# Two convolution layers and two SwiGLU layers on one core: the first filter block in two transfers, weight sums in other buffers, and a new instruction order

## The chip, the core and the metric

The kernel runs on one core of a Trainium2 chip. The core has five engines that run at the same time, each with its own list of instructions: TensorE (PE in the profile, its weight loads PEld) multiplies matrices and transposes, VectorE (DVE) and ScalarE (ACT) work element by element, GpSimd (POOL) does small things, SyncE (SP) issues DMA transfers. An instruction waits for semaphores that other engines and transfers raise. TensorE writes to PSUM, eight banks of 128 x 512 fp32; all other tiles are in SBUF, 128 partitions wide.

The metric is the time of one execution in microseconds (us) on the device; a smaller one is better. A version is shown by the median of its runs. A profile is taken of one execution apart from these.

## The reference

Two kinds of layer alternate, A, B, A, B, with the same weights both times, on x of 2048 rows by 512 columns (bf16):

```python
def _A_ref(q, k, v, shift_k, ssm_k, ssm_D):      # S = 2048, D = 512
    k_shift = sum(k_pad[:, t:t + S] * shift_k[:, 3 - t] for t in range(4))
    kv = k_shift * v
    y = irfft(rfft(kv, 2 * S) * rfft(ssm_k, 2 * S))[:, :S]   # a causal convolution per column
    return q * (y + kv * ssm_D)
def _B_ref(x, w_gate, w_up, w_down):             # F = 1792
    return (silu(x @ w_gate) * (x @ w_up)) @ w_down
x = A_q
x = x + _A_ref(_layernorm(x), A_k, A_v, ...)
x = x + _B_ref(_layernorm(x), ...)
x = x + _A_ref(_layernorm(x), A_k, A_v, ...)
x = x + _B_ref(_layernorm(x), ...)
```

The convolution y does not depend on x: it is made once and used by both A layers.

## The kernel before

**Tiling.** The 2048 rows are four blocks c of 512; in a block, row 4p + r stands on partition p in slot r. The convolution is a block convolution in the frequency domain. For each block of the filter (h) and of kv, TensorE multiplies the four slots with a table of cosines and sines (`fwd`), VectorE combines the results in butterflies, multiplies spectra (`product`), and TensorE goes back with the transposed table `inv`. kv itself is made on TensorE for the first two blocks: k, transposed, times 16 diagonal matrices `dg` that hold the taps (`shift_mul`), and then a product with v on VectorE (L614, L605). The filter lies with its columns on partitions, so TensorE transposes it for blocks 0 and 1 (`transpose_h`, L567) into the tile hs, and DMA does it for blocks 2 and 3.

**Units.** An FFN unit is (layer, block, half of the block): 16 units of 256 rows. Ahead of a unit, `prologue` normalises x, adds the A layer, normalises again to z and has z transposed to zT, by a DMA (L980), and for the first unit by TensorE (L1008). A unit reads zT against `w_gate` and `w_up` (L400, banks pf), ScalarE takes silu and copies (L1113, L1114, L1173, L1177), VectorE multiplies both, and TensorE multiplies the result with `w_down` (L1200, banks pd). In five late units the down product goes by a scheme of seven products in place of eight (`seven`, L1075); for it VectorE forms five sums and differences of halves of `w_down` once (`weight_sums`, L1022), each 128 x 1792.

**Buffers.** Tiles come from rings (L376), each with a number of equal buffers: one for h, one for k, one for v, one for hs, 11 of 8 KB a partition in s8, and so on. A new tile waits until the last reader of the tile that held its buffer is through.

**Order.** All instructions are recorded first, some 1,700 steps of them. The list `ORDER` (L55) gives each step its rank, and they are emitted in that sequence, engine by engine; it was found by a search outside the kernel. `Plan.walk` estimates when each step runs. From this, `Plan.issue` puts 33 filler matmuls of 128 columns (`warm`, L1482), which compute nothing, into TensorE's early waits, where the estimate has a wait of over 0.5 us before a limit, 6.0 us; what is left of the 33 goes to the first such place. The start of SP's queue is h block 0 (L432), k (L442), v (L472), x (L476), h block 1, v block 1, `w_gate`; k is on TensorE's list behind h: 16 transposes for h (L567), 16 for k (L456), then the pairs of matmuls on hs and the shift matmuls with `dg`.

The start of SP's queue and of TensorE's list, as the program is built:

```
SP:  hn (512 KB), kn, vt, xc, hn block 1, vt block 1, wg_sb, inv x2, kTb, wu_sb, wd_sb, wd_sb, xc
PE:  21 wm, 4 taps, 12 wm, 4 x 4 h transposes, 16 k transposes, 8 on hs, 8 on dg, ...
```

Of the kernel before, what the change touches and what calls it, by code (L numbers as in the profile page):

```python
# [9 lines left out]
P = 128  # L10
# [36 lines left out]
H_SPLIT = False  # L47
# [75 lines left out]

PASSES, WARM, FETCH, PHASE, TOOK = 4, 33, 256, 173, 1.1

NS = 8
BLOCKS = [("C", 0, 1), ("C", 1, 1), ("C", 2, 1), ("C", 3, 1),
# [1389 lines left out]
```

## Time and profile before

| | us |
|---|---|
| median of 3 runs | 339.34 (339.18 to 339.55) |
| profiled execution | 340.1 |
| its span, first to last instruction | 338.3 |
| TensorE busy, of the span | 333.9 |
| VectorE busy | 299.8 |
| ScalarE busy | 265.0 |
| first FFN matmul starts | 33.22 |
| one matmul of 512, 256, 128 columns behind another | 0.216, 0.109, 0.056 |

The span holds all instructions of the program; the 1.8 us between it and the execution's time lie around it. A matmul's row shows more than its share (0.379 us for 512 columns), since the next one starts before it is done; so a time for many is taken from start to start. A step of the chain that ended last says when it began, for how long, engine, tile and line.

### The profile page before, as it was taken

How to read it: one execution, taken by the hardware profiler on the slowest of the kernel's cores; microseconds unless marked ns; L12 is line 12 of the kernel's file. 1: busy time of each engine (PE TensorE's matmuls, PEld its weight loads, DVE VectorE, ACT ScalarE, POOL GpSimd, SP SyncE). 2: the span in 40 equal slices, each digit the busy share in tenths (PEclk: the TensorE clock that was granted, in tenths of full speed). 3: DMA queues.
4: the chain of work that ended last, by engine and by line, in shares of the span. 5: the costliest groups of instructions: out<-in, count | busy, mean ns of one | idle time of the engine just before them, and what ended most of it. 6: DMA issues, size and time to landing. Idle time of an engine off the chain costs nothing.

```text
span 338.3 us, 5940 instructions
## 1 busy us (share of the span) xinstructions
PE 333.9 (99%) x2172; PEld 205.7 (61%) x2172; DVE 299.8 (89%) x508; ACT 265.0 (78%) x543; POOL 34.5 (10%) x48
## 2 busy tenths in 40 slices
PE   9999999999999999999999999999999999999996
PEld 8665865645454564745444564644546587867884
DVE  7899999999779997999999999989997967977465
ACT  6989999999987477989999886989765555566473
POOL 4010011003100000132030000101200010100000
PEclk9999999999999999999999999999999999999999
DMA  7999501443355336381333263510504230203201
GB/s 266 341 290 365 75 0 33 84 107 90 64 125 93 81 79 155 62 159 32 62 48 67 57 107 116 105 34 16 96 16 96 56 85 2 48 17 78 64 3 62
DMA packets 77992, 31.59 MB, mean 93 GB/s; under 512 B 69765, under 2 KB 75786, under 8 KB 77962
## 3 DMA queue, kind: packets, MB, share of 16 engines
q1 hardware_dynamic: 77808, 31.13, 39.8%
q8 instruction: 17, 0.28, 0.3%
q14 instruction: 13, 0.11, 0.1%
q10 hardware_dynamic: 154, 0.07, 0.1%
HBM read 12.33 MB, written 2.10 MB: 43 GB/s over the span
## 4 chain that ended last, share of the span: by engine, by line
PE 87%; ACT 7%; DVE 5%; issue 1%; POOL 0%; DVEq 0%; POOLq 0%
PE pf L400 50%; PE pd L1200 17%; PE ps L1075 7%; PE ps L400 7%; PE ps L548 2%; ACT jk L922 2%; PE wm L1485 1%; PE ps L879 1%; ACT sg L1113 1%; ACT hr L1114 1%; ACT X L509 1%; PE pt L567 1%; DVE t L746 1%; DVE m L630 1%; DVE Z L750 1%; DVE t L742 1%
## 5 line engine op out<-in xcount | busy, mean ns | idle before, releaser
L400 PEld LDWEIGHTS <-zT 128*128 128x128 bf16 x528 | 51.5, 98 | 59.4 <-DMA zT<-z 0.9
L400 PE MATMUL pf<-wu_sb,zT 128*128 128x512 bf16 x264 | 65.0, 379 | 0.0
L400 PE MATMUL pf<-wg_sb,zT 128*128 128x512 bf16 x264 | 64.9, 379 | 0.0
L1200 PE MATMUL pd<-wd_sb,sg 128*128 128x512 bf16 x200 | 49.4, 379 | 0.0
L1113 ACT ACTIVATE sg<-pf 128x512 bf16<-128x512 f32 x66 | 38.7, 604 | 11.4 <-PE pf L400 10.3
L400 PE MATMUL pf<-zT,wg_sb 128*128 128x256 bf16 x368 | 46.7, 273 | 0.0
L1114 ACT CAST hr<-pf 128x512 bf16<-128x512 f32 x66 | 38.2, 591 | 9.6 <-PE pf L400 9.0
L400 PE MATMUL pf<-zT,wu_sb 128*128 128x256 bf16 x368 | 45.4, 273 | 0.2 <-ACT zT L1013 0.2
L742 DVE TENSOR_TENSOR t<-X,G 128x4096 bf16<-128x4096 bf16 x18 | 41.0, 2280 | 0.1
L400 PEld LDWEIGHTS <-wg_sb 128*128 128x128 bf16 x368 | 36.0, 98 | 8.0
L400 PEld LDWEIGHTS <-wu_sb 128*128 128x128 bf16 x368 | 36.0, 98 | 7.1 <-issue 0.5
L1173 ACT ACTIVATE sg<-pf 128x512 bf16<-128x512 f32 x46 | 27.5, 606 | 10.9 <-PE pf L400 9.7
L1177 ACT CAST ht<-pf 128x512 bf16<-128x512 f32 x46 | 27.3, 599 | 10.8 <-PE pf L400 10.4
L889 POOL TENSOR_TENSOR rstd<-mv,nhalf 128x2 f32<-128x2 f32 x20 | 18.5, 928 | 160.3 <-DVE mv L899 160.3
L1200 PEld LDWEIGHTS <-sg 128*128 128x128 bf16 x200 | 19.6, 98 | 21.5
L1200 PE MATMUL pd<-wd_sb,ht 128*128 128x512 bf16 (+1 forms) x126 | 29.1, 369 | 0.0
L898 DVE BATCH_NORM_STATS2 bst<-xc 128x6 f32<-128x512 bf16 x40 | 26.4, 682 | 0.5
L1180 DVE TENSOR_TENSOR ht<-ht,sg 128x512 bf16<-128x512 bf16 (+1 forms) x31 | 16.7, 546 | 9.5 <-ACT sg L1173 6.2
L889 POOL TENSOR_TENSOR rstd<-ve,nhalf 128x2 f32<-128x2 f32 x12 | 12.4, 1032 | 112.3 <-ACT ve L926 112.3
L1120 DVE TENSOR_TENSOR hr<-hr,sg 128x1024 bf16<-128x1024 bf16 x27 | 18.4, 681 | 4.3 <-ACT hr L1114 2.3
L509 ACT ACTIVATE X<-ps 128x512 bf16<-128x512 f32 x32 | 18.8, 611 | 2.2 <-DVE Z L746 1.1
L1200 PEld LDWEIGHTS <-ht 128*128 128x128 bf16 x126 | 12.3, 98 | 12.8 <-ACT z L945 0.3
(143 smaller groups left out, 525.7 us busy)
## 6 DMA issues: line engine op xcount, KB each, us to landing
hn<-in_A_ssm_k_dram SPq DMA_DIRECT2D x4, 512.0 KB, 4.0
vt<-in_A_v_dram SPq DMA_DIRECT2D x4, 512.0 KB, 6.0
xc<-in_A_q_dram SPq DMA_DIRECT2D x4, 512.0 KB, 5.3
out_dram<-xc SPq DMA_DIRECT2D x15, 128.0 KB, 1.8
wg_sb<-in_B_w_gate_dram SPq DMA_DIRECT2D x1, 1792.0 KB
wu_sb<-in_B_w_up_dram SPq DMA_DIRECT2D x1, 1792.0 KB, 7.9
wd_sb<-in_B_w_down_dram SPq DMA_DIRECT2D x1, 1280.0 KB, 13.2
sg<-hr SPq DMA_TRANSPOSE x66, 2.4
```

What stands on the lines that cost most here:

```text
L400: nc.tensor.matmul(o, lhsT=lhsT, rhs=rhs, start=(n == 0), stop=(n == len(terms) - 1))
L509: add("ACT", act(D), lambda: nc.scalar.activation(out=view(), in_=ps.t[:], func=ACT.Copy, scale=scale), r=[ps], w=[(buf, keys)], conv=conv)
L742: dve(8 * D, lambda t=t, part=part: nc.vector.tensor_mul(out=t.t[:], in0=x.t[:, :, part:part + 1, :].to_broadcast((P, R, 2, D)), in1=g.t[: ...
L889: add("POOL", cost, lambda: nc.gpsimd.tensor_tensor(out=rstd.t[:], in0=var(), in1=nhalf.t[:].to_broadcast((P, n)), op=ALU.pow), r=reads + ...
L898: add("DVE", 0.6, lambda st=st, i=i: nc.vector.bn_stats(out=st.t[:, 0:6], in_=xs[c].t[:, i, :]), r=[(xs[c], (i,))], w=[st])
L1075: nc.tensor.matmul(bank.t[:, half_ * C:(half_ + 1) * C], lhsT=lhsT(i), rhs=rhs(i), start=(first and i == 0 and half_ == 0), stop=(last and ...
L1113: add("ACT", act(D), lambda ps=ps, dst=dst, o=o, which=which: nc.scalar.activation(out=rows(dst, o), in_=ps.t[:], func=ACT.Silu) if which ...
L1114: out=rows(dst, o), in_=ps.t[:], func=ACT.Silu) if which == "g" else nc.scalar.copy(out=rows(dst, o), in_=ps.t[:]),
L1120: dve(n * W, lambda: nc.vector.tensor_mul(out=hr.t[:], in0=hr.t[:], in1=sg.t[:]), [sg], [hr], due=(unit, k / pairs, 0.0, "h"))
L1173: add("ACT", act(D), lambda ps=ps, o=o, sg=sg: nc.scalar.activation(out=sg.t[:, o:o + 2, :], in_=ps.t[:], func=ACT.Silu), r=[ps], w=[(sg, ...
L1177: add("ACT", act(D), lambda ps=ps, o=o, ht=ht: nc.scalar.copy(out=ht.t[:, o:o + 2, :], in_=ps.t[:]), r=[ps], w=[(ht, (o // 2,))], due=(uni ...
L1200: nc.tensor.matmul((pds[o] if not cs.start else pds[HP]).t[:, cs], lhsT=ht.tiles(q, o), rhs=wt["d"].t[:, ft, cs], start=(ft == std0 and no ...
```

## The change

Three things are changed, and no computation is added or left out.

First, `H_SPLIT` is set: `load_h` issues block 0 of the filter as two transfers of two column blocks each (256 KB), and `transpose_h` turns each row slot in two steps of two transposes, so that the steps on one half need that half alone. The functions held this branch before.

Second, the sums of the down weights are five tiles in place of three, in the buffers of h, k, hs, the diagonals, and one of s8 (three of s8 before). The diagonals `dg` are a ring of one buffer for this.

Third, `Plan.walk` lets TensorE run at half rate before 5.4 us of its own time, the limit for filler matmuls is 32.0 in place of 6.0, and `ORDER` is another list.

```diff
-H_SPLIT = False
+H_SPLIT = True
...
 ORDER = [
-    1, 64, 179, 187, 2, 5, 0, 11, 15, 3, 4, 8, 14, 34, 36, 9, 7, 10, 6, 13,
+    4, 91, 145, 160, 1, 7, 5, 10, 25, 0, 3, 14, 2, 6, 58, 59, 11, 9, 12, 8,
...
-PASSES, WARM, FETCH, PHASE, TOOK = 4, 33, 256, 173, 1.1
+PASSES, WARM, FETCH, PHASE, TOOK, RAMP = 4, 33, 256, 173, 1.1, 5.4
...
             o.end = o.start + o.cost
+            if o.eng == "PE" and o.start < RAMP:
+                o.end += 0.48 * min(1.92 * o.cost, RAMP - o.start)
...
-    dg = whole("dg", [P, KD, KS, P], parts=KD * KS)
+    dg = new("dg", "dg", [P, KD, KS, P], parts=KD * KS)
...
-        a = ws["14"] = new("s8", "wsa", [P, 2, NF // 2, C], parts=2)
-        b = ws["3"] = new("s8", "wsb", [P, NF // 2, C])
-        c = ws["67"] = new("s8", "wsc", [P, NF, C])
...
+        a0, a1 = (new(ring, "wsa", [P, NF // 2, C]) for ring in ("h", "k"))
+        b = new("hs", "wsb", [P, NF // 2, C])
+        c0, c1 = (new(ring, "wsc", [P, NF // 2, C]) for ring in ("dg", "s8"))
+        ws.update({"1": a0, "4": a1, "3": b, "6": c0, "7": c1})
+        for out, x0, x1, op in ((a0, lambda: ev(lo), lambda: od(hi), ALU.add), (b, lambda: ev(hi), lambda: od(hi), ALU.subtract),
+                                (a1, lambda: od(lo), lambda: ev(lo), ALU.subtract), (c0, lambda: ev(lo), lambda: ev(hi), ALU.add),
+                                (c1, lambda: od(lo), lambda: od(hi), ALU.add)):
...
-        plan.issue(*plan.order(ORDER), 6.0, warm)
+        plan.issue(*plan.order(ORDER), 32.0, warm)
```

The built program has the same number of matmuls, of steps on ScalarE and of DMA transposes; SP issues one transfer more. Its start:

```
SP:  hn blocks 2-3, kn, hn blocks 0-1, vt, xc, hn block 1, vt block 1, wg_sb, inv x2, kTb, wu_sb, wd_sb, hn, vt, wd_sb, xc
PE:  22 wm, 4 taps, 5 wm, 8 h transposes, 8 h transposes, 16 k transposes, 10 on hs, 4 on dg, ... 1 on hs, 6 wm, 16 on dg, ...
```

More of the change, by code (lines that the diff above doesn't have):

```diff
@@ L374, in span @@
         return slice(rows[0], rows[-1] + 1, rows[1] - rows[0])
-    plan = Plan({"h": 1, "k": 1, "v": 1, "hs": 1, "x": 2, "y": 2, "s8":11, "n": 2, "jk": 1, "dn": 1, "ks": 2, "z": 3, "zT":3,
+    plan = Plan({"h": 1, "k": 1, "v": 1, "hs": 1, "dg": 1, "x": 2, "y": 2, "s8":11, "n": 2, "jk": 1, "dn": 1, "ks": 2, "z": 3, "zT":3,
                  "ht":7, "st": 4, "bn": BN_SLOTS, "mv": 9, "ve": 8, "rs": 6, "pf": 4, "pc": 2, "pd": 2, **RINGS})
@@ L1027, in weight_sums @@
         lo, hi = slice(0, C), slice(C, D)
-        a = ws["14"] = new("s8", "wsa", [P, 2, NF // 2, C], parts=2)
-        b = ws["3"] = new("s8", "wsb", [P, NF // 2, C])
-        c = ws["67"] = new("s8", "wsc", [P, NF, C])
-        for out, keys, x0, x1, op in (
-                (lambda: a.t[:, 0], [(a, (0,))], lambda: ev(lo), lambda: od(hi), ALU.add),
-                (lambda: b.t[:], [b], lambda: ev(hi), lambda: od(hi), ALU.subtract),
-                (lambda: a.t[:, 1], [(a, (1,))], lambda: od(lo), lambda: ev(lo), ALU.subtract)):
-            dve(NF // 2 * C, lambda out=out, x0=x0, x1=x1, op=op: nc.vector.tensor_tensor(out=out(), in0=x0(), in1=x1(), op=op),
-                [wd], keys)
-        for n in range(2):
-            sl = slice(n * NF // 2, (n + 1) * NF // 2)
-            dve(NF // 2 * C, lambda sl=sl: nc.vector.tensor_tensor(out=c.t[:, sl], in0=wd.t[:, sl, lo], in1=wd.t[:, sl, hi], op=ALU.add),
-                [wd], [c])
+        a0, a1 = (new(ring, "wsa", [P, NF // 2, C]) for ring in ("h", "k"))
[5 more added lines that the diff above has]
+                                (c1, lambda: od(lo), lambda: od(hi), ALU.add)):
+            dve(NF // 2 * C, lambda out=out, x0=x0, x1=x1, op=op: nc.vector.tensor_tensor(out=out.t[:], in0=x0(), in1=x1(), op=op),
+                [wd], [out])
     def strided(src, off, dims):
@@ L1060, in seven @@
         for bank, rd, terms in (
-                (e, [ht, ws["14"], ws["3"]], (
-                    (0, lambda i: ht.tiles(2 * i + 1, 1), lambda i: ws["14"].t[:, 1, f0 + i]),
+                (e, [ht, ws["4"], ws["3"]], (
+                    (0, lambda i: ht.tiles(2 * i + 1, 1), lambda i: ws["4"].t[:, f0 + i]),
                     (1, lambda i: ht.tiles(2 * i, 0), lambda i: ws["3"].t[:, f0 + i]))),
@@ L1066, in seven @@
                     (1, lambda i: cb.t[:, 1, i], lambda i: wd.t[:, 2 * (f0 + i), 0:C]))),
-                (r, [(cb, (1,)), ws["67"]], (
-                    (0, lambda i: cb.t[:, 3, i], lambda i: ws["67"].t[:, 2 * (f0 + i) + 1]),
-                    (1, lambda i: cb.t[:, 2, i], lambda i: ws["67"].t[:, 2 * (f0 + i)]))),
-                (o, [(cb, (2,)), ws["14"]], (
-                    (0, lambda i: cb.t[:, 4, i], lambda i: ws["14"].t[:, 0, f0 + i]),))):
+                (r, [(cb, (1,)), ws["6"], ws["7"]], (
+                    (0, lambda i: cb.t[:, 3, i], lambda i: ws["7"].t[:, f0 + i]),
+                    (1, lambda i: cb.t[:, 2, i], lambda i: ws["6"].t[:, f0 + i]))),
+                (o, [(cb, (2,)), ws["1"]], (
+                    (0, lambda i: cb.t[:, 4, i], lambda i: ws["1"].t[:, f0 + i]),))):
             def go(bank=bank, terms=terms):
```

128 rows, old and new, of the table ORDER are left out of this document.

## The prediction

> **What bounds the kernel now.** I read the page's table of engines first, then the chain of waits in order of time, then busy time by stretches, and last the timelines of the queues and of VectorE for the first 34 us.
>
> ```profile
> PE 333.9 (99%) x2172; PEld 205.7 (61%) x2172; DVE 299.8 (89%) x508; ACT 265.0 (78%) x543; POOL 34.5 (10%) x48
> ```
> ```profile
> 0.77 2.40 PE wm L1485 x21
> 3.39 1.39 PE wm L1485 x12
> 4.78 1.71 PE pt L567 x16
> 6.49 1.20 PE pt L456 x16
> 7.69 7.03 PE ps L400 x80
> ...
> 31.49 0.70 ACT ks L604
> 32.20 0.50 ACT Yk L799
> 32.70 0.48 ACT zT L1013
> 33.22 5.40 PE pf L400 x48
> ...
> 250.95 1.30 DVE Z L647 x2
> 252.29 0.61 PE ps L400 x2
> ...
> 333.96 1.32 PE pd L1200 x12
> ```
> ```profile
> 31.30:34.00 2.70, 2.22 (x19) 1.35 (x19) 2.53 (x5) 2.70 (x7) 0.00 (x0) 1.00 1.06 364
> 34.00:335.30 301.30, 301.17 (x1872) 182.59 (x1869) 269.65 (x436) 235.54 (x482) 28.87 (x30) 1.00 0.34 68
> 335.30:338.30 3.00, 0.00 (x0) 0.00 (x0) 0.21 (x1) 0.37 (x1) 0.00 (x0) 0.96 0.41 125
> ```
>
> TensorE is the bound, and its work is fixed. The groups by shape give 978 matmuls 512 wide, 973 of 256 and 217 of 128; back to back they start 0.216, 0.109 and 0.056 us apart, so 211 + 106 + 12 = 329.4 us. The span of 338.3 is 0.8 before the first one, 329.4, a tail of 3.2 behind the last, and 4.9 in which TensorE starts nothing. Of these 4.9, about 3.0 are the start: until 7.0 us the matmuls stand 0.107 apart instead of 0.056 (1.71 us for 16 transposes; the same 16 take 0.9 later). About 1.0 is the hole before the first FFN matmul: the chain leaves TensorE at 31.3 and returns at 33.22, 1.9 us that hold 0.9 us of its work. Small holes at 26.3 and 26.9 are 0.2. Between 34 us and the end only three holes are left, at 150.9, 242.5 and 252.3 us, together 0.5. So a new order can win 1.7 us behind the start, no more.
>
> The hole at 31 to 33 us waits for the vector chain, which runs without a break worth the name from 16.65 us to the normalised rows z:
>
> ```profile
> 11.88 2.70 DVE L614 TENSOR_TENSOR vt<-ps,vt 128x512 bf16<-128x512 f32 x4 [0.18 <-PE ps L400]
> 15.44 0.69 DVE L537 TENSOR_TENSOR G<-ev 128x1024 bf16<-128x1024 bf16 x1 [0.26 <-ACT ev L509]
> 16.65 1.28 DVE L732 TENSOR_TENSOR t<-X,G 128x1024 bf16<-128x1024 bf16 x2
> 31.31 0.74 DVE L950 TENSOR_SCALAR z<-xc,mv,rstd 128x512 bf16<-128x512 bf16 x2 [0.26 <-POOL rstd L889]
> ```
>
> **The start.** The first h is issued at 0.74 and lands 3.6 us later, at 4.3; k is issued at 1.25 and takes 4.3, to 5.55.
>
> ```profile
> 0.74 0.45 SPq L432 DMA_DIRECT2D hn<-in_A_ssm_k_dram  x1
> 1.25 0.48 SPq L442 DMA_DIRECT2D kn<-in_A_k_dram  x1
> ```
>
> The new order on SP's queue is: h column blocks 2 and 3 (256 KB), k (512 KB), h blocks 0 and 1 (256 KB), then v, x and the rest. The second half of h thus goes behind k. The megabyte of h and k is the same, so this half should land when k landed, at 5.55. Bounds: 4.3 if it overtakes k, 6.0 with SP's additional issue of 0.45 on top; I take 5.55, because k, v and x land one after another here. The queue behind them (v at 1.79, x at 2.25) is issued 0.45 later, but v lands at 7.8 and is first used at 11.88.
>
> TensorE now runs 22 filler matmuls, the taps, 5 fillers: 6 fewer than before, so it reaches h 6 x 0.107 = 0.64 earlier, at 3.94. Eight transposes of the first half go to 4.79, then it waits 0.8 for the second; eight more end at 6.45; the 16 of k, at 0.107 to 7.0 and at 0.056 behind it, end at 7.6. Before, that was 7.53. All four hs rows need both halves, so the copies to SBUF start no earlier: VectorE's first at 6.1, as before. The split by itself: +0.1 on this path (from -0.35, if the half lands at 4.3, to +0.5).
>
> **Behind it, to the first FFN.** In the new order seven of the eight pairs on hs stand ahead of the last shift matmuls; before, six. One pair is 2 x 0.216 = 0.43. The shift matmuls, which ended at 13.69, end at 13.69 + 0.1 + 0.43 = 14.2. The last of the four products of L614 follows its bank, 14.4 to 15.1, where it ended at 14.58. One butterfly of G (0.6) has moved in front of these products; three are left behind: 15.1 + 3 x 0.6 = 16.9 until the spectral products of L732, against 16.65. From there to z the two orders hold the same instructions on VectorE, so z comes 0.25 late, and with it the first FFN matmul, 33.22 to 33.47. Queued behind z are the transposes (L1008) and their two copies (L1013, L1011); SP is not in it.
>
> Six of the 33 filler matmuls now stand in the middle of this stage, between hs and the third shift group: 6 x 0.056 = 0.33. They cost nothing while TensorE waits for z anyway (the hole of 1.0); with that cover gone they cost 0.33.
>
> **The sums of the down weights.** Five subtractions and additions of 128x1792 before and after, 1.08 us each by the rows of L1035 and L1039. Only the buffers change: h, k, hs, the diagonals, and one s8 slot instead of three. Those buffers have had their last reader by 175 us of TensorE work, the sums are read first at about 252. 0, and two more s8 slots for products and banks.
>
> **SP further on.** The third h and v (1 MB) are now issued ahead of the larger part of the down weights, whose landing (20.3 + 13.2 = 33.5) moves by about 2.6 us to 36; its first reader stands behind 42 us. If a read were at 34 it would cost 2. 0.
>
> **The order from 34 us on.** The matmuls are the same. I added up, for each of the 16 FFN units, TensorE's work ahead of its first use of zT and the work ahead of z on the engine that writes it. At eight of them, among these the ones with the least slack (second, third, eleventh to thirteenth), the lead of the row read first shrinks by at most 0.4. Where it shrinks by more, it eats about the slack that there was. The fourth unit's first row: TensorE comes 1.5 earlier while z does not, and the slack was 1.4 (issued 84.91, 2.4 to land by the page, read at 88.71). The sixth loses 6.8 of 6.8, the fifteenth 2.1 of 2.0, the sixteenth 1.7 of 1.7, always by the row that has least. So these reads come about as the rows land, by nothing to spare. The three old holes can go (-0.5) or three or four of 0.3 can come (+1.0). I take 0, nearer the lower end, as most of the lists are this much alike.
>
> **Sum.** +0.1 + 0.15 + 0 + 0 + 0 + 0 = +0.25. The profiled execution took 340.1 (span 338.3 and 1.8 around it), the median of the three runs is 339.34; the sum on the execution is 340.35, and against the median 339.6.
>
> **Rivals.**
> Faster. The second half overtakes k and the order is as good as its search: TensorE is through k's transposes at 7.2, z comes 0.35 early, the holes of 0.5 go, and a little of the one at 26. For it: only 0.5 of 301 us behind 34 are holes, so good orders exist. Against: k, v, x land in turn. 339.34 - 0.35 - 0.5 - 0.1 = 338.4.
>
> Slower, by the clock. In the profiled execution the spacing fell to 0.056 at 7.0 us, 6.2 us after the first matmul; the one hole on the way is 0.24, before the taps. The change puts one of 0.8 at 4.8 us. If the full rate needs unbroken work, it comes later: by nothing, or, if counting starts anew at 5.6, at 11.8, which is 4.8 us more at half rate, 2.4 lost. Seven to fourteen us is where the shift matmuls feed VectorE, so all of it reaches z. I take 1.5, over the middle, as the stretch from 0.8 with its small hole did not raise the clock by 3.5 either: 339.6 + 1.5 = 341.1. It decides if the hole is over some tenths. [...]
>
> Slower, by the order. zT is read within 0.1 to 0.5 of its landing at most units, so small errors of the search become holes: three of 0.35 more, 340.6.
>
> That the split does not bring h earlier is in the forecast already.
>
> **Chances.** Forecast (339.1 to 340.0) 0.41; faster 0.28; clock 0.16; order 0.15. With 0.2% (0.68 us), which is about what can be told from no change here: faster 0.28, within 0.41, slower 0.31. The range for 8 in 10 reaches into the cases on both sides, 338.1 to 341.3; the likeliest case alone is 339.1 to 340.0.
>
> **What would show it.** Right: a hole in TensorE from 4.8 to 5.5; spacing 0.056 from 7 us; the products of L614 ending near 15.1 and L732 starting near 16.9; first FFN matmul at 33.3 to 33.7; under 0.8 us of holes behind 34. Wrong: the second half of h landing under 5 us, or spacing still 0.107 at 8 us, or holes of over 1 us behind 34, above all at the fourth unit's first matmul near 87.

## The result, and the profile after

The changed kernel takes 343.55 us (median of 4; 343.17 to 343.66) against 339.26 (339.14 to 339.55) for the kernel before: 1.0123 times as long, 95% interval 1.0106 to 1.0141. The range of the prediction ended at 341.3. The profiled execution took 343.2 with a span of 341.4, 3.1 longer than the profiled span of before; what lies around the span is the same 1.8 us.

The page's table of engines shows TensorE's work unchanged (31 of its records are missing in this trace):

```profile
PE 333.0 (98%) x2141; PEld 205.4 (60%) x2172; DVE 299.5 (88%) x508; ACT 263.3 (77%) x543; POOL 35.7 (10%) x48
```

The chain of waits, in order of time, begins in another way (start, duration, what). Before, it ran over fillers on TensorE to the transposes of h at 4.78, without a DMA. Now a transfer of h holds it until 7.75:

```profile
1.75 6.00 DMA hn<-in_A_ssm_k_dram
...
7.79 1.04 PE pt L569 x8
8.84 1.71 PE pt L458 x16
```

The second half of h is issued at 1.75 and lands 6.0 us later. The 16 transposes of k behind it take 1.71, 0.107 each: TensorE is still at half rate at 10 us; before, the spacing fell to 0.056 at 7.0. The clock record of the trace puts the full rate at 10.49. (The column of the granted clock in the views shows 1.00 for the time ahead of the record's first entry; at half rate the spacing of the rows shows it.) The same transposes of k on TensorE's timeline, before and after; the chain above lets each step begin where the one before it ends, so its starts are later:

```profile
6.29 1.40 PE L456 MATMUL pt<-ident,kn 128*128 128x128 bf16 x16
```
```profile
8.63 1.91 PE L458 MATMUL pt<-ident,kn 128*128 128x128 bf16 x16
```

Busy time by stretches, the three that answer to those shown of before (PE, PEld, DVE, ACT, POOL, granted clock, DMA share, GB/s):

```profile
34.20:36.90 2.70, 2.70 (x22) 1.52 (x21) 2.69 (x6) 2.57 (x7) 0.00 (x0) 1.00 1.44 343
36.90:338.30 301.40, 299.79 (x1845) 182.28 (x1869) 269.16 (x435) 233.44 (x482) 30.22 (x30) 1.00 0.33 66
338.30:341.30 3.00, 0.00 (x0) 0.00 (x0) 0.24 (x1) 0.37 (x1) 0.00 (x0) 1.00 0.40 128
```

The long stretch and the tail have the lengths they had; they only begin later. From the first FFN matmul to the last matmul it is 301.93 us, and was 301.78. The first FFN matmul moved from 33.22 to 36.10. So 2.88 of the 3.03 us by which the last matmul is late are lost ahead of it.

VectorE's timeline shows where they enter (in brackets the idle time before, and what ended it):

```profile
8.23 0.42 DVE L585 COPY hs<-pt 128x512 bf16<-128x512 bf16 x1 [3.56 <-PE pt L569]
...
15.87 2.03 DVE L616 TENSOR_TENSOR vt<-ps,vt 128x512 bf16<-128x512 f32 x3 [0.20 <-PE ps L402]
...
19.62 1.93 DVE L734 TENSOR_TENSOR t<-X,G 128x1024 bf16<-128x1024 bf16 x3
...
34.21 0.73 DVE L952 TENSOR_SCALAR z<-xc,mv,rstd 128x512 bf16<-128x512 bf16 x2 [0.25 <-POOL rstd L891]
```

The first copy of hs starts 2.13 late (6.10 before), the spectral products 2.97 late (16.65, then L732), z 2.90 late (31.31). The loss is complete by 20 us.

### The profile page after: what moved, and what is told of

The parts are those of the page before. It is cut to its first block, busy times and chain, and to the rows that moved or that the text cites. A ratio compares the mean times of both kernels' runs of the same rounds, so it can differ in the third digit from the quotient of the medians.

```text
span 341.4 us, 5909 instructions
## 1 busy us (share of the span) xinstructions
PE 333.0 (98%) x2141; PEld 205.4 (60%) x2172; DVE 299.5 (88%) x508; ACT 263.3 (77%) x543; POOL 35.7 (10%) x48
## 4 chain that ended last, share of the span: by engine, by line
PE 77%; DVE 8%; DMA 5%; issue 3%; ACT 3%; POOL 2%; SPq 2%; POOLq 0%; DVEq 0%
PE pf L402 47%; PE pd L1198 17%; PE ps L1073 7%; PE ps L402 5%; DMA wd_sb<-in_B_w_down_dram 2%; DMA hn<-in_A_ssm_k_dram 2%; POOL rstd L891 2%; DVE m L632 1%; SPq L446 1%; ACT jk L924 1%; DVE t L744 1%; DVE bst L900 1%; ACT sg L1111 1%; DMA zT<-z 1%; DVE G L673 1%
## 5 line engine op out<-in xcount | busy, mean ns | idle before, releaser
L402 PE MATMUL pf<-wg_sb,zT 128*128 128x512 bf16 x254 | 64.0, 379 | 0.5
L402 PE MATMUL pf<-wu_sb,zT 128*128 128x512 bf16 x258 | 64.2, 380 | 0.3
L1198 PE MATMUL pd<-wd_sb,sg 128*128 128x512 bf16 x191 | 46.9, 379 | 0.5
L402 PE MATMUL pf<-zT,wu_sb 128*128 128x256 bf16 x368 | 46.4, 273 | 0.2
L891 POOL TENSOR_TENSOR rstd<-mv,nhalf 128x2 f32<-128x2 f32 x20 | 16.3, 818 | 153.8 <-DVE mv L901 144.1
L891 POOL TENSOR_TENSOR rstd<-ve,nhalf 128x2 f32<-128x2 f32 x12 | 16.0, 1332 | 120.6 <-ACT ve L928 120.6
```

Of the source, the lines that this page charges most:

```text
L402: nc.tensor.matmul(o, lhsT=lhsT, rhs=rhs, start=(n == 0), stop=(n == len(terms) - 1))
L891: add("POOL", cost, lambda: nc.gpsimd.tensor_tensor(out=rstd.t[:], in0=var(), in1=nhalf.t[:].to_broadcast((P, n)), op=ALU.pow), r=reads + ...
L1198: nc.tensor.matmul((pds[o] if not cs.start else pds[HP]).t[:, cs], lhsT=ht.tiles(q, o), rhs=wt["d"].t[:, ft, cs], start=(ft == std0 and no ...
```

## The experiments

All edits are against the changed kernel or the kernel before, as named. "Full rate" is the time at which the trace's clock record has TensorE leave half rate. Beside each median stands the ratio of the means to runs of the kernel before on the same chip, with its 95% interval.

**k behind both halves.** The changed kernel with its second and third transfer exchanged:

```
-        plan.issue(*plan.order(ORDER), 32.0, warm)
+        seq, place, when = plan.order(ORDER)
+        at = {o.n: i for i, o in enumerate(seq)}
+        seq[at[11]], seq[at[13]] = seq[at[13]], seq[at[11]]
+        plan.issue(seq, place, when, 32.0, warm)
```

> The changed kernel with k issued behind the second half of h instead of between the halves. Theory (the second half is late because it stands behind k): it lands near 5.0 us instead of 7.75, TensorE has no hole of more than 0.3 us behind its fillers, the full rate is there near 7.0 instead of 10.5, the first FFN matmul starts at 33.2 to 33.7 instead of 36.1; 339.0 to 340.2. Rival (a load in two pieces is slow by itself, or the rest of the change costs the time): the second half lands after 6 us, or the FFN starts after 35; 342 or more.

341.95 (340.85 to 343.17), 1.0081 (1.0057 to 1.0104). The second half landed at 4.66, as expected, but k at 7.07, and the hole is now in front of k's transposes, 1.34 us. In the traced execution, the fastest, the full rate came at 5.71 and the first FFN matmul at 33.70; the others reach as far as the changed kernel. So the place behind k is not all of it: the hole had moved. Neither forecast of the time holds.

**One transfer.** The changed kernel, all of h at the place of the first half:

```
-   ... q.dma_start(out=hn[b].t[:, sl], in_=h3[:, sl, 0:L]) ...
+   ... q.dma_start(out=hn[b].t[:], in_=h3[:, :, 0:L]) if n else None ...
```

> The changed kernel with all of the first h in one transfer, at the place of the first half; the order of all other instructions, the weight sums and the fillers stay. Theory (the whole loss comes from the two transfers): h lands near 4.3, full rate at 7.0, first FFN matmul at 33.0 to 33.7; 338.8 to 339.9. Rival (the searched order or the weight sums cost behind 34 us): 341 or more, with holes of over 1 us there.

341.56 (341.14 to 341.76), 1.0056 (1.0041 to 1.0071): neither theory. Behind the first FFN matmul nothing is lost (302.02 to the last), so the rival falls. But the FFN starts at 34.66, with the full rate at 9.74. TensorE's timeline has the reason:

```profile
3.43 0.72 PE L1483 MATMUL wm<-const-bfloat16-1.0 128*128 128x128 bf16 x5
4.82 1.89 PE L569 MATMUL pt<-ident,hn 128*128 128x128 bf16 x16 [0.67 <-DMA hn<-in_A_ssm_k_dram]
6.50 1.91 PE L458 MATMUL pt<-ident,kn 128*128 128x128 bf16 x16
```

The six fillers that the change took from the front leave a hole even when h comes whole: 0.85 us from where the next matmul could have started.

**The same with the fillers back.** One transfer, 22 and 11 fillers ahead of h, none in the middle of the stage:

```
-                warm(*fill[o])
+                warm(*fill[o][:2], {22: 22, 5: 11, 6: 0}[fill[o][2]])
```

> The changed kernel with all of the first h in one transfer, and its fillers ahead of h as before: 33 there (22 and 11) and none in the middle of the stage. With one transfer alone the time was still 2 us above before, and TensorE had a hole of 0.85 us ahead of h, the full rate at 9.7. Theory (what was left is this hole, by the clock): no hole over 0.3 us up to 10 us, full rate between 4.2 and 7.6, first FFN matmul at 32.9 to 33.7, within 0.3% of the kernel before. Rival (the order, the weight sums or the transfers further on cost it): 0.4% or more above before, the FFN after 34 or holes of over 1 us behind it.

339.50 (339.39 to 340.14), 0.9999 (0.9990 to 1.0007): the time of before.

```profile
3.43 1.36 PE L1483 MATMUL wm<-const-bfloat16-1.0 128*128 128x128 bf16 x11
4.69 1.90 PE L569 MATMUL pt<-ident,hn 128*128 128x128 bf16 x16
6.38 1.26 PE L458 MATMUL pt<-ident,kn 128*128 128x128 bf16 x16
```

Full rate at 6.80, seen in k's 16 transposes; spectral products at 16.68, first FFN matmul at 33.15. This kernel holds the new order, the weight sums in their new buffers and the transfers further on. Together they cost nothing that can be measured.

**The hole filled, the transfers kept.** First with 24 more fillers ahead of the second half:

```
             ...
+            if o.n == 39:
+                warm('pc', 1, 24)
             o.emit()
```

> The changed kernel with 24 more filler matmuls ahead of the first transpose of the second half, so that the hole of 2.7 us is filled; the transfers stay. Theory (part of the loss is the clock, set back by the hole): full rate at 7.0, second half still at 7.75, the transposes of h and k done near 9.2 instead of 10.4; the FFN starts about 1.2 earlier; 342.0 to 342.7. Rival (only the landing counts, or the rate does not ask for unbroken work): the spacing is still 0.107 up to 10 us; 343.3 to 343.8.

343.64 (342.81 to 345.28), 1.0125 (1.0094 to 1.0155). By the time alone the rival wins; the trace says otherwise. The full rate came at 6.96 and the first FFN matmul at 34.41, 1.7 earlier than in the changed kernel (the second half landed at 6.24 here). But from there to the last matmul it took 304.15, 2.2 more. Most of that is one hole of 1.78 in TensorE's timeline (1.62 of it idle; another of 0.83 is at 319 us), and the DMA view of 241 to 246 us has an instruction fetch in it:

```profile
245.52 0.82 PE L404 MATMUL pf<-wg_sb,zT 128*128 128x512 bf16 x3 [1.62 <-DMA zT<-z]
```
```profile
q8 instruction: 1, 0.02, 1.2%
...
zT<-z SPq DMA_TRANSPOSE x2, 3.6
```

The same stretch of the changed kernel has no fetch, and its zT transposes land in 2.4 us:

```profile
q1 hardware_dynamic: 1854, 0.45, 44.5%
...
zT<-z SPq DMA_TRANSPOSE x2, 2.4
```

The 24 fillers are 48 more instructions in TensorE's stream, and the fetches come earlier in the work; one, at 243.46, fell on a transpose that is read just in time. In the other 13 traces that fetch comes behind these transposes, at 244.99 or later, and they land in 2.4 to 2.5 us. No run moved the fetch alone. So the experiment was repeated with the count kept: the six fillers of the middle of the stage, each 512 wide, in front of the second half:

```
-                warm(*fill[o])
+                warm(*fill[o][:2], 0 if fill[o][2] == 6 else fill[o][2])
+            if o.n == 39:
+                warm('pc', 1, 6, 512)
...
-    def warm(ring, slot, n):
-        t = psp.tile([P, P], F32, name="wm", tag=f"{ring}{slot}")
+    def warm(ring, slot, n, w=P):
+        wide = nc.const_aps.tensor(1.0, [P, w], BF16)
+        t = psp.tile([P, w], F32, name="wm", tag=f"{ring}{slot}")
...
-            nc.tensor.matmul(t[:], lhsT=ones, rhs=ones, start=True, stop=True)
+            nc.tensor.matmul(t[:], lhsT=ones, rhs=wide, start=True, stop=True)
```

> The changed kernel with its 6 fillers from the middle of the stage put ahead of the second half of h, each 512 instead of 128 wide: 2.6 us of filling at half rate with no more instructions than before, so that the fetches of instructions further on stay where they were (the 24 additional fillers moved one onto a zT transpose and lost 1.8 us there). Theory (the hole costs by the clock): full rate before 8, first FFN matmul 34.0 to 34.7, 341.6 to 342.4. Rival (the landing is all): 343.2 to 343.8.

340.81 (340.28 to 341.62), 1.0038 (1.0023 to 1.0054), better than the theory asked, and far from the rival's time. From the first FFN matmul to the last it is 301.90 again.

```profile
4.31 0.64 PE L571 MATMUL pt<-ident,hn 128*128 128x128 bf16 x8 [0.16 <-DMA hn<-in_A_ssm_k_dram]
4.79 1.47 PE L1486 MATMUL wm<-const-bfloat16-1.0 128*128 128x512 bf16 x6
6.22 0.64 PE L571 MATMUL pt<-ident,hn 128*128 128x128 bf16 x8
```

The second half landed at 6.17 here, the full rate was there at 4.10, and the FFN started at 33.27. Since the landing was earlier too than the 7.75 of the profiled execution, this run alone does not separate the hole from the landing; the next two kernels do.

**A hole in the kernel before.** Its second batch of 12 fillers, left out whole and by half, nothing else touched:

```
-                warm(*fill[o])
+                warm(*fill[o][:2], 0 if fill[o][2] == 12 else fill[o][2])
```

> The kernel before without its second batch of 12 filler matmuls, so that TensorE has a hole of about 1.1 us, from 3.5 to 4.6, and nothing else is touched. Theory (a hole sets the clock back): full rate near 10.4 instead of 7.0, 3.4 us at half rate, 1.7 lost; 340.5 to 341.3. Rival (this much idle time does not set it back): full rate at 7.0 and 339.2 to 339.5.

341.07 (340.17 to 342.07), 1.0044 (1.0029 to 1.0060); full rate at 9.04 in the traced execution, first FFN matmul 34.23. The theory's time holds (its switch was to come near 10.4): idle time alone, with every transfer as before, costs 1.4 us.

> The kernel before with 6 of its second batch of 12 filler matmuls left out: a hole of about 0.6 us, from 4.0 to 4.6. Theory (only a hole of about 1 us or more sets the clock back: in the changed kernel the 3.5 us ahead of the full rate hold a hole of 0.8): full rate at 7.0 and 339.2 to 339.5. Rival (any hole does): full rate near 10.4, 340.5 to 341.3.

(With 6 in place of the 0.) 340.15 (339.17 to 341.45), 1.0014 (0.9999 to 1.0029): not settled by the median. The traced execution is the slowest of the ten, 341.45, with the full rate at 9.88 and the FFN at 34.62; the fastest are as fast as before. So with a hole of 0.64 us the full rate came at 9.88 in the one execution that was traced, against 7.00 and 5.06 in the two traces without the hole; by the times it was not late in all.

**The changed kernel traced twice more, the kernel before once more.**

> The changed kernel once more, beside the others of this call and for a second trace. [...] The second half of h lands between 6.2 and 7.8. The median is 1.0 to 1.4% above before.

> The changed kernel a third time, for its start. The two traces so far have the full rate at 10.5 (343.2 us) and at 5.0 (340.8), and the nine executions of the second call fall in two groups, 340.3 to 340.9 and 342.2 to 344.2. [...] Rival (the rate follows the work alone): between 5.5 and 8.5, or an early rate with a time of 342 or more.

> The kernel before once more, for a second trace of it: how far the time of the full rate, the landings and the first FFN matmul differ between two executions. The profiled execution took 0.8 more than the median. If the start does that, the full rate or the first FFN matmul is up to 0.8 earlier here; if not, they stand within 0.1 of 7.0 and 33.2.

Nine more executions of the changed kernel: 340.35, 340.83, 340.84, 342.17, 343.39, 343.39, 343.56, 343.79, 344.19 (median 343.39; 1.0086, 1.0059 to 1.0114); on another chip, one of 344.32. The three traces:

| execution, us | second half of h lands | full rate | first FFN matmul |
|---|---|---|---|
| 340.83 | 6.68 | 5.02 | 33.76 |
| 343.17 | 7.75 | 10.49 | 36.10 |
| 344.32 | 7.84 | 12.53 | 37.16 |

TensorE's timeline, first of the 340.83 execution, then of the 344.32 one:

```profile
4.37 0.92 PE L569 MATMUL pt<-ident,hn 128*128 128x128 bf16 x8 [0.22 <-DMA hn<-in_A_ssm_k_dram]
6.72 0.64 PE L569 MATMUL pt<-ident,hn 128*128 128x128 bf16 x8 [1.43 <-DMA hn<-in_A_ssm_k_dram]
7.20 1.06 PE L458 MATMUL pt<-ident,kn 128*128 128x128 bf16 x16
```
```profile
4.57 1.04 PE L569 MATMUL pt<-ident,hn 128*128 128x128 bf16 x8 [0.42 <-DMA hn<-in_A_ssm_k_dram]
7.89 1.04 PE L569 MATMUL pt<-ident,hn 128*128 128x128 bf16 x8 [2.28 <-DMA hn<-in_A_ssm_k_dram]
8.72 1.91 PE L458 MATMUL pt<-ident,kn 128*128 128x128 bf16 x16
```

The same program, and the second batch of eight takes 0.64 or 1.04. Between the last two executions of the table the landing differs by 0.1 and the full rate by 2.04; the FFN differs by 1.06. A us at half rate cost about half a us at the FFN here: k's transposes start 0.09 later in the last execution, half rate lasts 1.95 longer behind that start, and the FFN moves by the 0.09 and 0.97 more. Of the first expectation the landing holds (6.68 in the 340.83 execution), and so does the median (343.39 against 339.47, 1.2% above). The 344.32 execution speaks against a rate that follows the work alone: full rate at 12.53, not between 5.5 and 8.5. The second trace of the kernel before has the full rate at 5.06 and k landing at 6.33, 0.75 later than in the profiled one; the FFN stands at 32.97 and the span is 338.3 again. So neither half of its expectation holds: the start moves too, by less, and the 0.8 that the profiled execution took above the median stays unexplained.

**Two and four transfers in the kernel before,** all ahead of k:

```
+        def go():
+            for sl in (slice(2, 4), slice(0, 2)) if b == 0 else (slice(0, 4),):
+                q.dma_start(out=hn[b].t[:, sl], in_=h3[:, sl, b * L:(b + 1) * L])
-        return add(eng, 0.62, lambda: q.dma_start(out=hn[b].t[:], ...
+        return add(eng, 0.62, go, ...
```

> The kernel before with its first h loaded by two transfers of 256 KB, one right behind the other and both ahead of k; nothing else is touched. Theory (two small transfers are slower than one, whatever stands between them): the last of h lands at 4.6 or later and k at 6.1 or later, v after 8; 340 to 341.5. Rival (only the place behind k was bad): h at 4.3 to 4.5, k at 5.6 to 6.0, 339.2 to 339.9.

342.32 (340.44 to 343.73), 1.0075 (1.0048 to 1.0102). The times show that two transfers are slower by themselves. The landings show little of it: h was complete at 4.93, k at 6.31, v at 8.11, where the six traces with one transfer have 4.32 to 4.77, 5.58 to 6.33 and 7.09 to 8.00. The traced execution, 340.51, has a hole of 0.4 ahead of h and the full rate at 6.93; the later executions, up to 3.2 us slower, have no trace. In three of them (342.65, 343.71, 343.73) the mean granted clock is 0.995, as in five other slow ones of the kernels with two transfers; everywhere else in these runs it is 0.998 to 1.000. Of a span of 341.9 that would be some 3.4 us at half rate (2 x 0.005 x 341.9, an estimate); where in the span they lie is not shown, since none of these was traced.

> The kernel before with its first h loaded by four transfers of 128 KB ahead of k. With one transfer the six traces have moved 1.00 to 1.04 MB by 5 us, with two transfers 0.81 to 0.91. Theory (each further transfer costs the queue about the same, 0.3 to 0.6 us): about 0.5 to 0.7 MB by 5 us, h complete after 5.3, k after 7.0; 341.5 to 344. Rival (the cost is one of halves or of the place, not of the number): 0.8 MB or more by 5 us, k by 6.5.

340.84 (340.64 to 342.08), 1.0045 (1.0027 to 1.0063). The theory fails in part: h was complete at 4.71, no later than with two, and only k was late, 7.08; the 0.74 MB are between the two forecasts. The DMA view of the first 5 us says what had moved, in the kernel before, the changed kernel, and with two and four transfers:

```profile
DMA packets 678, 1.07 MB, mean 213 GB/s; under 512 B 30, under 2 KB 547, under 8 KB 678
```
```profile
DMA packets 484, 0.84 MB, mean 168 GB/s; under 512 B 34, under 2 KB 360, under 8 KB 484
```
```profile
DMA packets 628, 0.83 MB, mean 167 GB/s; under 512 B 37, under 2 KB 554, under 8 KB 628
```
```profile
DMA packets 638, 0.74 MB, mean 149 GB/s; under 512 B 69, under 2 KB 586, under 8 KB 638
```

By 5 us the kernels with one transfer of h have moved 1.03 to 1.07 MB in all six traces, those with two 0.83 to 0.93 in all seven, the one with four 0.74. At the 392 GB/s that the changed kernel's windows show from 7.0 to 10.4 us, the 0.2 MB between the first two are 0.5 us. What the queue does in that time was not found. The number of transfers alone does not give it, since four did not delay h.

## Why the prediction was wrong

The four kernels of one design show both parts of the loss, as ratios to before:

| | fillers leave a hole | hole filled |
|---|---|---|
| two transfers | 1.0123 and 1.0086 (the change) | 1.0038 |
| one transfer | 1.0056 | 0.9999 |

On the chip that ran three of the four, before took 339.47, the change 343.39, with its hole filled 340.81, and with one transfer and no hole 339.50. So filling the hole gains 2.6 of the 3.9 us by the medians, and 1.7 by the means (342.5 and 340.9), since the executions of the change lie in two groups. This is no clean split into hole and landing: in the two traces with the hole filled the second half landed at 6.24 and 6.17, in the three of the change at 7.75, 6.68 and 7.84, and no run shows whether that is chance.

The traces split it. Take the start of k's 16 transposes, add half of the time for which half rate lasts behind it (at 0.107 us a matmul, against 0.056, about half of the work is done in it), and subtract the sum from the start of the first FFN matmul. What is left is 26.53 to 26.59 us in all 14 traces, of the old order and of the new:

| execution | k's transposes start | half rate behind that | first FFN matmul | left |
|---|---|---|---|---|
| before | 6.29 | 0.71 | 33.22 | 26.58 |
| before, second trace | 6.38 | 0 | 32.97 | 26.59 |
| change, 340.83 | 7.20 | 0 | 33.76 | 26.56 |
| change, 343.17 | 8.63 | 1.86 | 36.10 | 26.54 |
| change, 344.32 | 8.72 | 3.81 | 37.16 | 26.54 |
| hole filled, 340.32 | 6.69 | 0 | 33.27 | 26.58 |
| one transfer, hole | 6.50 | 3.24 | 34.66 | 26.54 |
| one transfer, no hole | 6.38 | 0.42 | 33.15 | 26.56 |
| before, hole of 12 fillers | 6.35 | 2.69 | 34.23 | 26.53 |

So two things fix the start of the FFN. In the profiled execution of the change the later start of k's transposes, which stand behind the second half of h, costs 2.3 us and the longer half rate 0.6. In the 344.32 execution it is 2.4 and 1.55; in the 340.83 one 0.9, of which an early full rate gives back 0.4. With the fillers alone left out of the kernel before, it is 0.1 and 1.0.

- **The second half's landing: the step that failed first.** "This half should land when k landed, at 5.55", with 6.0 as the upper bound. In the five traces with k between the halves it was 7.75, 6.24, 6.68, 6.17 and 7.84. k itself landed at 5.50 to 5.84 there, so the half came behind k and not with it. The megabyte is the same, but less had moved by 5 us in each trace with h in pieces; why stays open. In the two latest, one or two of the transfer's 16 parts are far behind the rest: 14 had landed by 6.55 in the one, 15 by 6.51 in the other. Taking equal bytes for equal time had no row behind it: the trace of before shows the start with whole loads of 512 KB only. Its landing of k, 5.58, is also the earliest of the six traces with one transfer; in the others k landed between 5.81 and 6.33.
- **The first half.** The forecast let the first eight transposes begin at 3.94. The first half landed at 4.27 to 4.52 in the same five traces, the whole of h at 4.32 to 4.77 in the six with one transfer; the transposes began at 4.31 to 4.57, behind a wait of 0.3 to 0.6. So the split brought the front little or nothing.
- **The hole.** Forecast 0.8 us from 4.8 to 5.5; measured 2.6, 1.6 and 2.5 in the three traces of the change.
- **The rate.** The forecast kept the full rate at 7.0 and gave the clock 0.16. That rival had the order of events that the profiled execution shows: hole (2.6), later rate (10.49), VectorE's chain late (2.97 at the spectral products), z late (2.90). Its 1.5 is near what a hole alone cost at the FFN (1.0, 1.4 and 1.4 in the three traces that have one without a second transfer) and was 0.6 and 1.55 in two traces of the change; the late landing, the larger part in both, was not in it. It let the switch come at 7.0 or, with a count that starts anew behind the hole, at 11.8. The traces show no such fixed place: the changed kernel switched at 5.02, 10.49 and 12.53, the kernel before at 7.00 in one trace and at 5.06 in the other.
- **The six fillers.** The forecast booked their absence in front as 0.64 us gained, TensorE reaching h earlier. TensorE was free earlier and waited; with one transfer that wait alone costs 2.0 us (341.56 against 339.57). The other end of the move was right: the six in the middle cost nothing, the wait behind them is 0.34 in the changed kernel and 0.69 where they are gone.
- **One more hs pair, +0.15.** Not there at the FFN. In the kernel with one transfer and its fillers the products of L614 do end 0.39 late (14.97 against 14.58), about as forecast; but the three butterflies behind them run without the wait of 0.26 that stood there before, and the spectral products start at 16.68 (16.65 before), the FFN at 33.15 (33.22).
- **Weight sums, 0.** Right: five of 1.09 us as before (1.08), and nothing measurable in that kernel.
- **SP's order further on, 0.** Right: TensorE waits for no weight behind 34 us.
- **The order from 34 us on, 0.** Right: +0.15 (301.93 against 301.78, and the second trace of before has 302.05). The old holes (0.11, 0.14, 0.26) went and two came (0.30 near 66, 0.23 near 246); the one feared at 87 did not. The order rival falls.
- **The faster rival** needed the half to overtake k; it came 0.6 to 2.3 behind 5.55.

## What to carry to other kernels

In some executions here a wait of TensorE at half rate was paid twice, as the wait and as a later full rate: with a hole of 0.85 us and one transfer the full rate came at 9.74 and the FFN 1.4 late. So fillers that bridge a load are sized to the latest landing seen, not to the planner's, and a kernel's executions are looked at one by one, since one program switched at 5.02, 10.49 and 12.53. Cutting a load in two so that work may begin on the first half delayed the second here (6.17 to 7.84 with k between the halves, 4.32 to 4.77 for the whole load), and the first came hardly earlier (4.27 to 4.52): price the whole queue from a trace with the pieces in it. And an experiment that adds instructions to an engine can bring a fetch of them onto a just-in-time transfer further on (at 243.46 us here, with a hole of 1.78): keep the count, or its effect further on is mistaken for the thing tested.

## What the runs showed of the hardware

- The first switch to the full rate came, in 14 executions traced, between 4.10 and 12.53 us, in the same program at 5.02, 10.49 and 12.53, and in the kernel before at 5.06 and 7.00.
- In the profiled executions of both kernels full rate lasted 331.09 us by the clock record, with spans of 338.3 and 341.4. The two switches of the kernel before are 1.94 apart, those of the changed kernel up to 7.51: the place of the switch differs between executions of one program. What sets it was not shown.
- The switch came 2.70 us behind the end of the long wait in one execution of the changed kernel (7.79 and 10.49) and 4.64 behind it in another (7.89 and 12.53); in the third it came ahead of that wait, at 5.02. In the kernel before with its hole of 0.64 it came at 9.88 in the traced execution. How long a wait has to be to delay it was not shown.
- Once at full rate, TensorE kept it in two traces over waits of 1.6 us (the 340.83 execution, and four transfers, full at 4.63 and then idle ahead of k).
- With 48 instructions more at the start a fetch came at 243.46 us (244.99 or later in the other 13 traces), between the issue and the landing of two transposing transfers, which landed in 3.95 and 3.17 us, 2.4 to 2.5 in the other traces; with the count kept the hole was 0.22 instead of 1.78.
